# A PSUM buffer shared by feed-forward and spectral work: another engine frees it, and the spectral pieces stand at other places

## The chip, the cores and the metric

One core of one Trainium2 chip. The metric is the device time of the kernel in microseconds (us), median of several runs. PE is TensorE, PEld its weight loads, DVE VectorE, ACT ScalarE, POOL GpSimd, SP SyncE. Before and after are compared within the same rounds.

## The reference, cut to what matters

The reference returns an output and seven gradients of a gated mix of a spectral filter `a` and a GeGLU feed-forward block `b`:

```python
g = _sigmoid((x * gate_w).sum(-1, keepdims=True))
a = _A_ref(x, A_w_r, A_w_i)      # rfft2, times a complex weight, irfft2
b = _B_ref(x, B_w_gate, B_w_up, B_w_down)   # (gelu(x@w_gate) * (x@w_up)) @ w_down
return g * a + (1 - g) * b
# out: value, and by vjp the gradients of all inputs but B_x   (x: 2048 x 576, F = 4608)
```

The kernel has a first phase (18 groups of columns, 4 pairs of row blocks each: products z and x·w, the gate's elementwise work, weight gradients of an earlier group, and between them the spectral transforms as small "pieces") and a second phase of pure matrix products.

## The kernel before: the parts that matter

The PSUM tiles of the first phase make up eight banks, where a bank is 512 F32 per partition (a `[P, 2, 512]` tile is two). Four hold the x products (`ph`, two buffers of two banks), two hold weight gradients (`pw`), and the last two are one single buffer, `pz`. It serves z at the start of a pair and each spectral piece after the first group:

```python
pz = ps1.enter_context(tc.tile_pool(name="pz", bufs=1, space=PSUM))
...
def pftile():                       # PSUM of a spectral piece
    fctr[0] += 1
    if pw is None and fctr[0] % 2:  # first group only: a second buffer
        return pg.tile([P, 2, 512], F32, tag="pg", name="pf")
    return pz.tile([P, 2, 512], F32, tag="z", name="pf")
```

The last piece of the inverse transform (a product with the D table) read its two results from PSUM with ScalarE once and with VectorE twice:

```python
ev = unit([DF], F32, name="ev")                       # DF = 289
yo = unit([D], name="yo")
nc.scalar.activation(ev[:], yps[:, 0, :DF], ACT.Copy, scale=scale)
V.scalar_tensor_tensor(yo[:, 0:DF], yps[:, 1, :DF], scale, ev[:], op0=ALU.mult, op1=ALU.add)
V.scalar_tensor_tensor(yo[:, D - 1:DF - 1:-1], yps[:, 1, 1:DF - 1], -scale, ev[:, 1:DF - 1],
                       op0=ALU.mult, op1=ALU.add)
```

A pair of row blocks, from the second group on (`hs` are the halves of weight-gradient products, `fft_next()` emits one piece, `H_ew1`/`H_ew2` are the two parts of the gate's elementwise work):

```python
z, xy_full = H_mm(g, m)             # z into pz
xy = xy_full(0)                     # first x product
das = H_da(m, z)                    # four ScalarE reads free z
ta = H_ew1(xy)                      # ScalarE: q, xb, hu; VectorE: four instructions
for h in carry: h()
xy = xy_full(1)                     # second x product
fft_next()                          # first piece
tc_ = H_ew1(xy); H_ew2(g, 2 * m, ta, das[0])
hs[0]()
run_W(hs[1:], n - k, mid)           # other pieces by count, often the last one at the end
```

## Time and profile before

| | before |
|---|---|
| time, median (the runs that the prediction had) | 1579.02 us (1577.78 to 1581.86) |
| span of the profiled run | 1573.3 us |
| PE busy / idle | 1468.2 / 105.1 us |
| mean granted PE clock | 0.981 |

The lines of the page, of the stretches and of the waits are in the prediction below. They are read in this order: how busy PE is, in which stretch it is not, what it waits for there, and how one such wait comes about.

### The profile page before, as it was taken

How to read it: one execution, taken by the hardware profiler on the slowest of the kernel's cores; microseconds unless marked ns; L12 is line 12 of the kernel's file. 1: busy time of each engine (PE TensorE's matmuls, PEld its weight loads, DVE VectorE, ACT ScalarE, POOL GpSimd, SP SyncE). 2: the span in 40 equal slices, each digit the busy share in tenths (PEclk: the TensorE clock that was granted, in tenths of full speed). 3: DMA queues.
4: the chain of work that ended last, by engine and by line, in shares of the span. 5: the costliest groups of instructions: out<-in, count | busy, mean ns of one | idle time of the engine just before them, and what ended most of it. 6: DMA issues, size and time to landing. Idle time of an engine off the chain costs nothing.

```text
span 1573.3 us, 29838 instructions
## 1 busy us (share of the span) xinstructions
PE 1468.2 (93%) x11760; PEld 1074.2 (68%) x11760; DVE 844.5 (54%) x2243; ACT 685.5 (44%) x1355; POOL 22.3 (1%) x51
## 2 busy tenths in 40 slices
PE   7989999799999999989989888799998999999998
PEld 5657667567667666656656565576877777777776
DVE  6596676788767886655756556567113312121100
ACT  5576665566665766545655455466100000000000
POOL 1000000000000000000000000000000000000000
PEclk9999999899999999999999999999999999999999
DMA  5144434445444444432433334354999987778773
GB/s 181 50 120 114 119 106 124 122 120 157 125 131 124 122 118 119 121 111 77 122 103 111 107 91 114 100 144 122 257 203 217 203 167 163 161 168 159 157 152 70
DMA packets 503353, 210.47 MB, mean 134 GB/s; under 512 B 307595, under 2 KB 497068, under 8 KB 503212
## 3 DMA queue, kind: packets, MB, share of 16 engines
q1 hardware_dynamic: 499772, 202.83, 52.6%
q0 software_dynamic: 1632, 4.72, 1.0%
q8 instruction: 92, 1.51, 0.4%
q10 hardware_dynamic: 1808, 1.02, 0.2%
q14 instruction: 49, 0.40, 0.1%
HBM read 40.89 MB, written 93.82 MB: 86 GB/s over the span
## 4 chain that ended last, share of the span: by engine, by line
PE 56%; issue 23%; DVE 9%; ACT 5%; POOL 1%; DMA 1%; SPq 1%; POOLq 0%; DVEq 0%; ACTq 0%
PE xy L332 16%; PE wps L429 13%; PE z L320 9%; PE wps L412 5%; PE acc L909 3%; PE xy L327 2%; PE acc L951 2%; PE wps L442 2%; PE z L323 1%; PE pf L655 1%; PE pf L478 1%; ACT q L352 1%; DVE om L374 1%; DVE A L372 1%; ACT xb L353 1%
## 5 line engine op out<-in xcount | busy, mean ns | idle before, releaser
L332 PE MATMUL xy<-wgu,xT 128*128 128x512 bf16 x1152 | 264.8, 380 | 0.0
L951 PEld LDWEIGHTS <-pin 128*128 128x128 bf16 x2304 | 225.4, 98 | 56.8
L429 PEld LDWEIGHTS <-xn 128*128 128x128 bf16 x2304 | 225.8, 98 | 32.1 <-issue 0.2
L332 PEld LDWEIGHTS <-xT 128*128 128x128 bf16 x1152 | 106.9, 98 | 146.8 <-issue 32.1
L345 ACT ACTIVATE da<-z,omg 128x256 bf16<-128x256 f32 x288 | 113.3, 475 | 193.6 <-PE z L323 193.0
L320 PE MATMUL z<-wdT,dOT 128*128 128x256 bf16 x1152 | 150.3, 288 | 46.8 <-DVE yo L674 21.7
L355 DVE TENSOR_SCALAR s<-q 128x512 bf16<-128x512 bf16 x144 | 41.9, 291 | 237.3 <-ACT q L352 237.3
L320 PEld LDWEIGHTS <-dOT 128*128 128x128 bf16 x1152 | 116.7, 103 | 74.3 <-issue 31.5
L412 PE MATMUL wps<-dB,A 128*128 128x288 bf16 x1152 | 156.5, 286 | 0.0
L909 PE MATMUL acc<-wd_all,pin 128*128 128x288 bf16 x1152 | 143.7, 286 | 6.2 <-ACT f32t L914 4.5
L951 PE MATMUL acc<-wgT,pin 128*128 128x288 bf16 x1152 | 143.4, 286 | 0.0
L951 PE MATMUL acc<-wuT,pin 128*128 128x288 bf16 x1152 | 143.4, 286 | 0.0
L909 PEld LDWEIGHTS <-pin 128*128 128x128 bf16 x1152 | 112.6, 98 | 35.8 <-issue 5.7
L429 PE MATMUL wps<-dHg,xn 128*128 128x256 bf16 x1152 | 136.1, 274 | 0.0
L412 PEld LDWEIGHTS <-A 128*128 128x128 bf16 x1152 | 112.7, 98 | 29.8
L429 PE MATMUL wps<-dHu,xn 128*128 128x256 bf16 x1152 | 132.8, 273 | 0.0
L961 ACT COPY f32t<-acc 128x576 f32<-128x576 f32 x16 | 10.2, 639 | 249.1 <-PE acc L951 249.1
L352 ACT ACTIVATE q<-xy 128x512 bf16<-128x512 f32 x144 | 86.1, 598 | 65.5 <-PE xy L332 65.5
L963 DVE SCALAR_TENSOR_TENSOR f32t<-gwf,dlog,f32t 128x576 f32<-128x576 f32 x16 | 13.1, 818 | 186.6 <-ACT f32t L961 186.6
L364 ACT ACTIVATE om<-s 128x512 bf16<-128x512 bf16 x144 | 93.0, 646 | 3.3 <-DVE s L356 3.3
L365 ACT ACTIVATE s<-s 128x512 bf16<-128x512 bf16 x144 | 90.7, 630 | 4.6
L354 ACT CAST hu<-xy 128x512 bf16<-128x512 f32 x144 | 87.5, 608 | 0.0
(176 smaller groups left out, 1736.9 us busy)
## 6 DMA issues: line engine op xcount, KB each, us to landing
scr<-A SPq DMA_DIRECT2D x144, 128.0 KB, 1.8
scr<-dHg SPq DMA_DIRECT2D x144, 128.0 KB, 1.9
scr<-dHu SPq DMA_DIRECT2D x144, 128.0 KB, 1.9
out_dram<-dw SPq DMA_DIRECT2D x67, 128.0 KB, 2.1
wd_all<-in_B_w_down_dram SPq DMA_DIRECT2D x3, 1728.0 KB, 12.6
out_dram<-dwd SPq DMA_DIRECT2D x34, 144.0 KB, 1.9
scr_p<-Vt SPq DMA_DIRECT2D x32, 144.5 KB, 2.2
Vp<-scr_p SPq DMA_DIRECT2D x16, 289.0 KB, 3.1
```

Of the source, the lines that this page charges most:

```text
L320: nc.tensor.matmul(zo(t), lhsT=dOT[:, ci, t, :], rhs=wdT[:, ci, :], start=(t % 4 < 2 and ci == 0), stop=False)
L332: nc.tensor.matmul(xy[k][:, t % 2, :], lhsT=xT[:, ci, t, :], rhs=wgu[:, ci, :], start=False, stop=(ci == 3))
L345: nc.scalar.activation(da[:, tt, :], z[:, tt, k, :], ACT.Copy, scale=omg32[:, t:t + 1])
L352: nc.scalar.activation(q[:], hg, ACT.Square)
L354: nc.scalar.copy(hu[:], xy[:, :, FG:2 * FG])
L355: V.tensor_scalar(s[:], q[:], A_GELU, 1.0, op0=ALU.mult, op1=ALU.add)
L364: nc.scalar.activation(om[:], s[:], ACT.Sigmoid, scale=-2.0 * C_GELU)
L365: nc.scalar.activation(s[:], s[:], ACT.Sigmoid, scale=2.0 * C_GELU)
L412: nc.tensor.matmul(wps[:, :288], lhsT=tl(0, t)[:, fch * P:(fch + 1) * P], rhs=dB[:, t, h * 288:(h + 1) * 288], start=(t == 0), stop=(t == ...
L429: nc.tensor.matmul(wps[:, cc, :], lhsT=xn[:, t, (c0 + cc) * P:(c0 + cc + 1) * P], rhs=tl(k, t), start=(t == 0), stop=(t == T - 1))
L909: nc.tensor.matmul(bps[:, h, :288], lhsT=At[:, r, :], rhs=wd_all[:, fc, h * 288:(h + 1) * 288], start=(fc == 0), stop=(fc == NFC - 1))
L951: nc.tensor.matmul(xps[:, h, :288], lhsT=src[:, r, :], rhs=wT[:, h * 288:(h + 1) * 288], start=(k == 1 and f0 + r == 0), stop=(k == 2 and ...
```

## The change

The intent: z is freed by ScalarE alone and no longer by VectorE, whose queue is long (in the case at 681 us that the prediction shows, the gate's six instructions L371 to L376 ran ahead of VectorE's own two reads); and no piece stands right before the next z or right behind another piece. The core of the diff:

```diff
-                ev = unit([DF], F32, name="ev")
+                ev = unit([2, DF], F32, name="ev")
                 yo = unit([D], name="yo")
-                nc.scalar.activation(ev[:], yps[:, 0, :DF], ACT.Copy, scale=scale)
-                V.scalar_tensor_tensor(yo[:, 0:DF], yps[:, 1, :DF], scale, ev[:], ...)
-                V.scalar_tensor_tensor(yo[:, D - 1:DF - 1:-1], yps[:, 1, 1:DF - 1], -scale, ev[:, 1:DF - 1], ...)
+                nc.scalar.activation(ev[:], yps[:, :, :DF], ACT.Copy, scale=scale)
+                V.tensor_tensor(yo[:, 0:DF], ev[:, 0, :], ev[:, 1, :], op=ALU.add)
+                V.tensor_tensor(yo[:, D - 1:DF - 1:-1], ev[:, 0, 1:DF - 1], ev[:, 1, 1:DF - 1], op=ALU.subtract)
...
             das = H_da(m, z)
-            ta = H_ew1(xy)
+            q = H_q(xy)                       # only the first of the three ScalarE reads
+            if n:
+                fft_next()                    # first piece: between the two x products
+                n -= 1
+            ta = H_ew1(xy, q)
...
+                jobs = [(0, sig0)] * bool(carry) + carry + [(1.7, second)] + [(0, sig0)] * (not carry) + hs
+                us = sum(j[0] for j in jobs)
+                at, k, late = 0.0, 1, [sig1]
+                for w, f in jobs:             # w: 1.7 us for a w half or an x product, 1.0 for a d half
+                    if k <= n and at > 0 and at >= k * us / (n + 1) - 0.6:
+                        fft_next()
+                        k += 1
+                        if len(state) == 2 and late:
+                            late.pop()()      # second sigmoid block
+                    f()
+                    at += w
```

(Cut: `run_W` goes, every half carries its time, the first group keeps the order of its matmuls, where the first piece stood between the x products before too.)

More of the change, by code (lines that the diff above doesn't have):

```diff
@@ L347, in H_da, with H_q, H_ew1 @@
         return das
-    def H_ew1(xy):
-        xb, q, s, hu = (ewt(n) for n in ("xb", "q", "s", "hu"))
-        hg = xy[:, :, 0:FG]
-        nc.scalar.activation(q[:], hg, ACT.Square)
-        nc.scalar.copy(xb[:], hg)
+    def H_q(xy):
+        q = ewt("q")
+        nc.scalar.activation(q[:], xy[:, :, 0:FG], ACT.Square)
+        return q
+    def H_ew1(xy, q):
+        xb, s, hu = (ewt(n) for n in ("xb", "s", "hu"))
+        nc.scalar.copy(xb[:], xy[:, :, 0:FG])
         nc.scalar.copy(hu[:], xy[:, :, FG:2 * FG])
@@ L398, in W_units, with halves @@
         dwd_tiles, wp = {}, {}
-        def halves(f):
-            return [lambda: f(0), lambda: f(1)]
+        def halves(f, us):
+            return [(us, lambda: f(0)), (us, lambda: f(1))]
         def wtile(key):
@@ L422, in f @@
                     wst[0].dma_start(out_6[r0:r0 + P, :], dwd[:])
-            return halves(f)
+            return halves(f, 1.0)
         def u_dw(k, ov, c0):
@@ L435, in f @@
                 wst[0].dma_start(ov[:, c0:c0 + TPB, fsl], dw[:])
-            return halves(f)
+            return halves(f, 1.7)
         def tail(half):
@@ L449, in tail @@
             wst[0].dma_start(out_5[512:576, fsl], dw[HI, :])
+        tl_ = halves(tail, 1.0)
         w = [u_dw(k, ov, c0) for k, ov in ((1, o4v), (2, o5v)) for c0 in range(0, 4, TPB)]
@@ L452, in W_units @@
         if g == 0:
-            return [[w[0], halves(tail)], [w[1], d[0]], [d[1], d[2], d[3]], [w[2], w[3]], []]
-        return [[d[0]], [d[1], w[0]], [d[2], d[3], halves(tail)], [w[1], w[2]], w[3]]
+            return [[w[0], tl_], [w[1], d[0]], [d[1], d[2], d[3]], [w[2], w[3]], []]
+        return [[d[0]], [d[1], w[0]], [d[2], d[3], tl_], [w[1], w[2]], w[3]]
     side = []
@@ L669, in f @@
                                          start=(lc == 0), stop=(lc == 2))
-                ev = unit([DF], F32, name="ev")
+                ev = unit([2, DF], F32, name="ev")
                 yo = unit([D], name="yo")
-                nc.scalar.activation(ev[:], yps[:, 0, :DF], ACT.Copy, scale=scale)
-                V.scalar_tensor_tensor(yo[:, 0:DF], yps[:, 1, :DF], scale, ev[:], op0=ALU.mult, op1=ALU.add)
-                V.scalar_tensor_tensor(yo[:, D - 1:DF - 1:-1], yps[:, 1, 1:DF - 1], -scale, ev[:, 1:DF - 1],
-                                       op0=ALU.mult, op1=ALU.add)
+                nc.scalar.activation(ev[:], yps[:, :, :DF], ACT.Copy, scale=scale)
+                V.tensor_tensor(yo[:, 0:DF], ev[:, 0, :], ev[:, 1, :], op=ALU.add)
+                V.tensor_tensor(yo[:, D - 1:DF - 1:-1], ev[:, 0, 1:DF - 1], ev[:, 1, 1:DF - 1], op=ALU.subtract)
                 LD.dma_start(dv[:, i, :], yo[:])
@@ L752, in early_loads @@
         LD.dma_start(gwb[:], gate_w.partition_broadcast(P))
-    def run_W(hs, n, mid=None):
-        total = max(len(hs), 1)
-        k = 0
-        for j in range(total):
-            while k < n and k * total <= j * n:
-                fft_next()
-                k += 1
-            if mid and 2 * j >= total - 1:
-                mid()
-                mid = None
-            if j < len(hs):
-                hs[j]()
-        while k < n:
-            fft_next()
-            k += 1
     carry, pend = [], None
@@ L797, with sig0, second, sig1 @@
             das = H_da(m, z)
-            ta = H_ew1(xy)
+            q = H_q(xy)
[3 more added lines that the diff above has]
+            ta = H_ew1(xy, q)
+            state = []
+            def sig0():
+                H_ew2(g, 2 * m, ta, das[0])
+                side_work()
+                state.append(None)
+            def second():
+                xy = xy_full(1)
+                state.insert(0, H_ew1(xy, H_q(xy)))
+            def sig1():
+                H_ew2(g, 2 * m + 1, state[0], das[1])
+                side_work()
             if g == 0:
+                second()
                 fft_next()
-            for h in carry:
-                h()
-            carry = []
-            xy = xy_full(1)
-            k = 1 if n and hs else 0
-            if k or g == 0:
-                fft_next()
-            tc_ = H_ew1(xy)
-            H_ew2(g, 2 * m, ta, das[0])
-            def mid():
-                side_work()
-                H_ew2(g, 2 * m + 1, tc_, das[1])
-                side_work()
-            if hs:
-                hs[0]()
-            if g == 0:
-                fft_next()
-                mid()
-            else:
-                run_W(hs[1:], n - k, mid)
+                sig0()
+                fft_next()
+                sig1()
+            else:
+                jobs = [(0, sig0)] * bool(carry) + carry + [(1.7, second)] + [(0, sig0)] * (not carry) + hs
[3 more added lines that the diff above has]
+                    if k <= n and at > 0 and at >= k * us / (n + 1) - 0.6:
+                        fft_next()
+                        k += 1
[3 more added lines that the diff above has]
+                    at += w
+                while k <= n:
+                    fft_next()
+                    k += 1
+                if late:
+                    sig1()
+            carry = []
             if pr == 1:
@@ L866 @@
     wst[0] = nc.scalar
-    for h in carry + [h for us in pend[:4] for u in us for h in u] + pend[4]:
+    for _, h in carry + [h for us in pend[:4] for u in us for h in u] + pend[4]:
         h()
```

## The prediction

Also cut is the working by which the two VectorE sums would cost the same from SBUF as from PSUM, a change of nothing in part (1); the trace before did not show that. The 0.45 to 0.46 us under "What would show it" is what they took before (0.458 and 0.449).

> **What bounds the kernel now.** I read the page's busy shares first, then the busy time by stage, then what the TensorE waits for, then one stretch of the timeline.
>
> ```profile
> span 1573.3 us, 29838 instructions
> PE 1468.2 (93%) x11760; PEld 1074.2 (68%) x11760; DVE 844.5 (54%) x2243; ACT 685.5 (44%) x1355; POOL 22.3 (1%) x51
> ```
>
> TensorE (PE) is busy for 93% of the span, so the kernel can gain by matmul time or by the 105 us (1573.3 - 1468.2) in which PE stands still. The change removes no matmul. So the question is where those 105 us lie. The stretches below are the ones where the work changes: head and forward transform (to 225), the spectral middle (225 to 600), the inverse transform (600 to 1050), the pairs without spectral work, the second phase. Columns: stretch, its length, then busy time of PE, PEld, VectorE (DVE), ScalarE (ACT), GpSimd, then granted clock, DMA share, GB/s.
>
> ```profile
> 0.00:110.00 110.00, 91.51 (x810) 63.80 (x811) 77.16 (x202) 69.56 (x126) 4.39 (x18) 0.95 0.41 121
> 110.00:225.00 115.00, 112.98 (x901) 80.35 (x899) 79.40 (x225) 73.53 (x147) 0.00 (x0) 1.00 0.37 103
> 225.00:600.00 375.00, 353.56 (x2785) 247.56 (x2784) 290.28 (x774) 237.10 (x477) 0.00 (x0) 0.98 0.45 130
> 600.00:1050.00 450.00, 399.95 (x3084) 278.43 (x3083) 274.35 (x760) 247.13 (x501) 0.00 (x0) 0.96 0.38 107
> 1050.00:1110.00 60.00, 60.00 (x494) 44.31 (x492) 43.46 (x121) 34.99 (x71) 0.00 (x0) 1.00 0.52 133
> ```
>
> The inverse stretch loses 450 - 399.95 = 50.0 us and the middle 375 - 353.56 = 21.4 us. Where no spectral piece is interleaved (1050 to 1110) PE is never idle: the feed-forward part alone saturates it. So the spectral pieces bring the idle time. The waits of PE from 200 to 1100 us say how (total us, times, longest):
>
> ```profile
> PE z L320 <- DVE yo L674: 21.7, 12, 4.9
> PE pf L655 <- DVE yo L674: 17.7, 12, 4.1
> PE z L320 <- ACT Vt L618: 12.3, 4, 8.0
> PE pf L667 <- DVE yo L674: 4.4, 2, 4.0
> PE z L320 <- ACT ZT L658: 3.8, 4, 1.4
> ```
>
> All are waits for one buffer: z, two PSUM banks held once and no second pair, which the z product of each pair of row blocks and every spectral piece take in turn. 21.7 + 17.7 + 4.4 = 43.8 us are waits for the second VectorE instruction that reads an inverse D result; the other lines of that view add up to 27.7 us, nearly all for a ScalarE evacuation that had only just begun because the piece stood right before the next z. One case:
>
> ```profile
> 681.36 0.40 ACT L672 ACTIVATE ev<-pf 128x289 f32<-128x289 f32 x1
> 681.50 0.42 DVE L371 TENSOR_TENSOR xb<-xb,s 128x512 bf16<-128x512 bf16 x1
> ...
> 683.88 0.46 DVE L673 SCALAR_TENSOR_TENSOR yo<-pf,ev 128x289 bf16<-128x289 f32 x1
> ...
> 684.25 0.45 DVE L674 SCALAR_TENSOR_TENSOR yo<-pf,ev 128x287 bf16<-128x287 f32 x1
> ...
> 684.85 1.44 PE L655 MATMUL pf<-Btab,Vp 128*128 128x256 bf16 x6 [4.11 <-DVE yo L674]
> ...
> 687.17 3.57 PE L320 MATMUL z<-wdT,dOT 128*128 128x256 bf16 x16 [0.89 <-ACT ZT L658]
> ```
>
> ScalarE had its half at 681.76. VectorE still had to run the gate's L371 to L376, six elementwise instructions, ahead of its two, so the bank came free at 684.70, 2.9 us later. And then the 16 z matmuls took 3.57 us; undisturbed they take 1.9. The wait is followed by slow matmuls.
>
> [...] granted clock 0.50 from 685 to 690 us after the 4.11 us wait, likewise after the 8.0 us one. In windows of 5 us, busy time times (1 - clock) sums to 3.1 us in the middle and 11.8 us in the inverse stretch: a second cost of the same waits. [...] the trace has 406 (ev) and 639 (128x576 f32 to f32, line L961). [...] 759 ns for 576 elements in the trace (L965) [...].
>
> **The change, part by part.** (1) Evacuation. Thirty-two ACTIVATEs of 289 elements become 32 of 578: 32 x (0.64 - 0.41) = 7.4 us more ScalarE, spread over 450 us in which ScalarE is busy 247. Both VectorE sums now read SBUF[...]. The gain is that z comes free at the end of the ACTIVATE. In the case above that is 681.36 + 0.64 = 682.0 instead of 684.7, 2.7 of the 4.11 us; at 705.41 and 844.73 (waits 2.17 and 2.06, release 3.2 and 2.7 us earlier) the whole wait. I take 85% of 43.8, 37 us, for this part alone, and most of the slow matmuls with it.
> (2) Spacing. A pair of row blocks carries two or three pieces (157 slots over 61 pairs). Before, the last often came at the end of the pair, right before the z of the next one, or two stood about 1 us of matmul apart. Now one goes between the two x products and the others at even times. Worked through with durations of the trace for a pair with d, w pieces of the weight gradients, from the start of z: z matmuls to 2.1, tail rows to 2.6, first x product to 4.34; da (four ACTIVATEs) frees z at 3.9, so the first piece runs 4.34 to 5.08 without a wait; ScalarE does q to 5.15 and the piece 5.28 to 5.95. Second x product to 6.8, half a d to 7.8, second piece 7.8 to 8.45 (z free since 5.95); ScalarE still has q, xb, hu of the second half (to 8.6) and two sigmoids (to 9.85), so it evacuates at 9.85 to 10.65. Third piece at 11.2 to 11.9, evacuated by 13.0; the next z at 13.65. No wait of PE is left, the smallest margin is 0.5 us. For the first pair of a group, with the carried product ahead of the second x product, the last evacuation ends at about 13.6 and the next z is due at 13.7: no margin, so some waits of a few tenths there.
> (3) Order of the gate work. The second sigmoid block moves behind a piece; in the seven pairs after the last piece it moves to the end of the pair. ScalarE then has its two sigmoids 1.3 us before the next da is due, which is 2.3 us after the next z starts; it fits. In those seven pairs VectorE finishes about 1 us after the next da. No gain, little loss.
> Sum: idle 50.0 + 21.4 and slow clock 11.8 + 3.1 give 86.3 us at most (1579 - 86 = 1493). I leave 5 us in the inverse stretch. In the middle VectorE is busy 290 of 375 us and would be at 80% of a stretch of 360, and the 8.0 us wait went back to ScalarE waiting 6.5 us for VectorE products (buffers used in a ring), which spacing softens only; I leave 10 of 24.5 there. The forward part (6.3 us of z waits before 225 us) keeps its order in the first group: nothing. Gain 57 + 14 = 71, less 4 for small new waits: 67, so 1512 us.
>
> **Rivals.** (a) ScalarE takes the place of VectorE as the late releaser: its queue holds q, xb, hu and sigmoids ahead of a piece, up to 3 us. For it: in the case above the ACTIVATE itself came 1.6 us after the last matmul of its piece. Against: ScalarE is 55% busy in the inverse stretch, and the worked pair hides that delay. If the buffer came free 0.3 us late at each of the 128 middle and inverse pieces, that would leave some 38 us: 1545. (b) VectorE becomes the bound in the middle, since 12 product instructions per 8 pieces lie on top of the gate work. For it: 290 of 375 us; against: 375 - 21 = 354 still leaves 18% free. Then the middle gains nothing: 1526. (c) The waits hide something else, a transfer or the weight-gradient banks, and PE stays idle for that: DMA share is 0.38 to 0.45 there and PE waits for DMA only 1.1 us, for weight-gradient banks 0.4 us; I give it little, at most 20 us: 1532. (d) Everything goes: 1493.
>
> **Range and chances.** 1512 us, 1496 to 1540 for 8 in 10: the low end is nearly all of the 86 us, the high end is rival (a). Two per cent faster is 1547, a gain of 32 us; part (1) alone is worth 37 by the working above. Faster 0.89, same 0.10, slower 0.01.
>
> **What would show it.** In the changed kernel: PE busy at 440 or more of each 450 us in the inverse stretch, which shrinks to about 393; no wait of PE for yo; at most 20 us of waits for z in all, those left named ScalarE; clock 1.00 there; ScalarE's ev at 0.64 and the yo sums at 0.45 to 0.46; matmul counts equal and the second phase still 463 us. I would be wrong if waits of z for ev, ZT or Vt rise to 30 us or more (rival a), if VectorE is over 90% busy in the middle (b), or if PE is idle for other names (c).

## The result, and the profile after

| | before | after |
|---|---|---|
| time, median of 4 | 1580.44 us (1577.78 to 1582.66) | 1493.9 us (1492.21 to 1497.43) |
| span of the profiled run | 1573.3 us | 1490.4 us |
| PE busy / idle | 1468.2 / 105.1 us | 1450.0 / 40.4 us |
| mean granted PE clock | 0.981 | 0.993 |

The ratio is 0.9456, 95% interval 0.9432 to 0.948. (A ratio is the mean time of one kernel's runs over that of the other's of the same rounds, so not quite the ratio of the medians.) The gain of 86.5 us is larger than the 67 predicted, and the time lies below the stated range.

The head of the page after:

```profile
span 1490.4 us, 29909 instructions
PE 1450.0 (97%) x11760; PEld 1071.2 (72%) x11760; DVE 843.6 (57%) x2243; ACT 698.2 (47%) x1355; POOL 22.3 (1%) x51
```

The instruction counts are the same. PE idle fell by 64.7 us, and PE busy fell by 18.2 us although it does the same 11760 matmuls. Together that is the whole 82.9 us between the two spans.

Where: the same stretches of work in both kernels, cut at the first piece of the middle, the first of the inverse, the last of the inverse and the last z. First the kernel before (columns as in the prediction):

```profile
232.50:618.00 385.50, 364.85 (x2887) 257.81 (x2888) 293.19 (x782) 239.81 (x482) 0.00 (x0) 0.98 0.45 129
618.00:1015.50 397.50, 349.92 (x2699) 243.65 (x2697) 242.67 (x672) 219.08 (x443) 0.00 (x0) 0.97 0.37 104
1015.50:1093.00 77.50, 75.03 (x592) 52.26 (x592) 54.67 (x153) 45.33 (x94) 0.00 (x0) 0.96 0.55 138
```

Then the kernel after:

```profile
230.00:597.00 367.00, 360.01 (x2869) 255.43 (x2867) 293.15 (x781) 241.70 (x482) 0.00 (x0) 0.99 0.46 132
597.00:932.00 335.00, 335.00 (x2700) 241.27 (x2698) 238.07 (x663) 226.44 (x438) 0.00 (x0) 1.00 0.44 123
932.00:1010.00 78.00, 78.00 (x626) 54.03 (x624) 59.11 (x164) 50.27 (x104) 0.00 (x0) 1.00 0.60 149
```

Some 2700 matmuls of the inverse stretch took 397 us and now take 335, with PE busy throughout. By the times of the boundary instructions themselves (232.5, 618.1, 1014.8 and 1093.0 us before; 230.0, 596.7, 931.4 and 1006.6 after) the head gained 2.5 us, the middle 18.9, the inverse transform 62.0, the pairs behind it 3.0. The second phase (from 1131.7 of 1573.3, from 1045.3 of 1490.4) lost 3.5. The sum is 82.9. Between these boundaries the middle has 2888 matmuls before and 2866 after: some 22 of them, an estimated 2.8 us at 0.12 to 0.13 us each, moved into the head and the pairs behind, so that the middle itself gained nearer 16. In the inverse stretch the counts agree (2697 and 2698).

What PE still waits for (total us, times, longest; the first five lines):

```profile
PE tp L285 <- DMA xn<-in_A_x_dram: 5.0, 1, 5.0
PE acc L914 <- DMA pin<-scr: 4.2, 2, 2.1
PE z L320 <- ACT Vt L622: 4.1, 1, 4.1
PE acc L914 <- ACT f32t L919: 3.8, 5, 0.8
PE pf L496 <- DVE Vt L502: 3.7, 3, 1.2
```

The waits for yo are gone. One long wait for z is left, in the middle. The wait for xn stands at the start of the kernel and was there before (4.8 us). A piece with D results in the inverse stretch, to be set beside the case at 681 us that the prediction shows (timeline: start, length, engine, line, what):

```profile
679.81 0.29 PE L671 MATMUL pf<-At,ZT 128*128 128x289 bf16 x1
...
680.37 0.66 ACT L676 ACTIVATE ev<-pf 128x578 f32<-128x578 f32 x1
...
682.61 0.45 DVE L677 TENSOR_TENSOR yo<-ev 128x289 bf16<-128x289 f32 x1
...
682.98 0.45 DVE L678 TENSOR_TENSOR yo<-ev 128x287 bf16<-128x287 f32 x1
...
683.86 1.92 PE L320 MATMUL z<-wdT,dOT 128*128 128x256 bf16 x16
```

VectorE is as late as before: its sums end at 683.43, 2.4 us after ev. But z was free at 681.03, and the next z starts at 683.86 with no wait in brackets and takes 1.92 us (granted clock 1.00 from 683 to 688 us), against 3.57 in the case before. In this stretch the length of VectorE's queue no longer matters to PE. In the head some waits for VectorE remain (Vt L502, 3.7 us).

### The profile page after: what moved, and what is told of

Its sections match the earlier page's. It is cut to its first block, busy times and chain, and to the rows that moved or that the text cites. A ratio compares the mean times of both kernels' runs of the same rounds, so it can differ in the third digit from the quotient of the medians.

```text
span 1490.4 us, 29909 instructions
## 1 busy us (share of the span) xinstructions
PE 1450.0 (97%) x11760; PEld 1071.2 (72%) x11760; DVE 843.6 (57%) x2243; ACT 698.2 (47%) x1355; POOL 22.3 (1%) x51
## 4 chain that ended last, share of the span: by engine, by line
PE 66%; issue 23%; DVE 2%; SPq 1%; ACT 1%; DMA 1%; POOL 1%; POOLq 0%; ACTq 0%; DVEq 0%
PE wps L432 16%; PE xy L332 16%; PE wps L415 9%; PE z L320 8%; PE acc L914 3%; PE wps L445 2%; PE xy L327 2%; PE acc L956 2%; PE pf L671 2%; PE z L323 1%; PE pf L659 1%; PE pf L482 1%; POOL out_dram L971 1%; POOL out_dram L924 0%; DMA scr_p<-Vt 0%
## 5 line engine op out<-in xcount | busy, mean ns | idle before, releaser
L332 PE MATMUL xy<-wgu,xT 128*128 128x512 bf16 x1152 | 271.5, 380 | 0.0
L320 PE MATMUL z<-wdT,dOT 128*128 128x256 bf16 x1152 | 140.2, 276 | 5.9 <-ACT Vt L622 4.1
L320 PEld LDWEIGHTS <-dOT 128*128 128x128 bf16 x1152 | 112.6, 99 | 24.2 <-issue 9.6
L966 ACT COPY f32t<-acc 128x576 f32<-128x576 f32 x16 | 10.2, 639 | 249.1 <-PE acc L956 249.1
L919 ACT COPY f32t<-acc 128x576 f32<-128x576 f32 x16 | 10.2, 640 | 172.0 <-PE acc L914 172.0
```

The source lines that it names most:

```text
L320: nc.tensor.matmul(zo(t), lhsT=dOT[:, ci, t, :], rhs=wdT[:, ci, :], start=(t % 4 < 2 and ci == 0), stop=False)
L332: nc.tensor.matmul(xy[k][:, t % 2, :], lhsT=xT[:, ci, t, :], rhs=wgu[:, ci, :], start=False, stop=(ci == 3))
```

## The experiments

Two explanations compete for the gain: the earlier release (A in the texts below counts each part at its own worth) and the places of the pieces. The first two runs do one part alone. The differences in us that follow are between medians of runs; the ratios to the kernel before, each from its own rounds, say the same. The four runs of the changed kernel spread over 5 us (1492.21 to 1497.43), and runs 3 to 8 come from other rounds than it, so a difference of 5 us or less to it (runs 3, 6 and 7) is not clear of noise.

**1. The evacuation alone**, on the order of before.

```diff
 # kernel before, with only this
-                nc.scalar.activation(ev[:], yps[:, 0, :DF], ACT.Copy, scale=scale)
+                nc.scalar.activation(ev[:], yps[:, :, :DF], ACT.Copy, scale=scale)
 # and the two tensor_tensor sums on ev in place of the two scalar_tensor_tensor
```

> Only the evacuation of the inverse D results, on the old order of pieces. Theory A (the waits for yo are worth what the prediction's part (1) says, 37 us, plus about 9 us of slow clock behind them): 0.970 to 0.975 of the kernel before, about 1535 us; no wait of TensorE for yo left, the 27 us of waits for ScalarE evacuations still there. Rival B (the spacing is what counts and covers the late VectorE too): 0.99 or more.

Measured 1532.81 us, ratio 0.9698 (0.9672 to 0.9723): 48 us gained, as theory A has it. The inverse stretch went from 396.7 to 350.4 us (first and last inverse piece at 620.5 and 970.9), the middle did not gain (385.6 to 387.1). What PE waits for in this kernel:

```profile
PE z L320 <- ACT Vt L618: 12.3, 4, 8.0
PE z L320 <- ACT Y L484: 6.3, 5, 1.7
PE z L320 <- ACT ZT L658: 5.5, 4, 1.5
...
PE z L320 <- ACT ev L672: 3.6, 3, 1.3
```

No yo any more. The waits for ScalarE evacuations of the kernel before stand unchanged (Vt 12.3, Y 6.3), and ev joins them where a D piece is the last of its pair.

**2. The places without the evacuation**: the changed kernel with the old evacuation. The new order of the gate work, part (3) of the prediction, is in it too.

```diff
 # changed kernel, with only this taken back
-                nc.scalar.activation(ev[:], yps[:, :, :DF], ACT.Copy, scale=scale)
+                nc.scalar.activation(ev[:], yps[:, 0, :DF], ACT.Copy, scale=scale)
 # and the two scalar_tensor_tensor that read PSUM in place of the two tensor_tensor
```

> Only the new places of the pieces and the new order of the gate work; VectorE still reads the D results from PSUM. Theory A: the waits for ScalarE (27 us) go, but VectorE still frees z about 3 us after ev, which the worked pair with its 0.5 to 0.7 us of margin can't hide: 20 to 30 us of waits for yo remain, 0.965 to 0.975, about 1532 us. Rival B: 0.95 to 0.955, at most 10 us of waits for yo. If A's two halves (46 and 48 us) add up to more than the 86 us measured, they overlap.

Measured 1523.92 us, ratio 0.9632 (0.9602 to 0.9661): 57 us gained, a little more than theory A, far from B. The waits of PE in its inverse stretch:

```profile
PE pf L659 <- DVE yo L678: 10.1, 5, 2.5
PE z L320 <- DVE yo L678: 8.8, 6, 2.4
```

So 18.9 us of the 43.8 us of waits for yo remain, just under the 20 to 30 expected. The middle takes 367.3 us, as in the changed kernel (366.7): its gain is from the places and the order, not from the evacuation. The inverse takes 364.8. There the evacuation alone removes 46.3 us, the places without it 31.9 and both 62.0, so 16 us could be had by either. In the whole kernel 48 + 57 = 105 for 86.5.

**3 and 4. Taking the release back by a known amount.** ScalarE does each evacuation twice, which frees z later and loads ScalarE more.

```diff
 # 3: D results only; 4: all four kinds of evacuation of the middle and inverse
-                nc.scalar.activation(ev[:], yps[:, :, :DF], ACT.Copy, scale=scale)
+                for _ in range(2):
+                    nc.scalar.activation(ev[:], yps[:, :, :DF], ACT.Copy, scale=scale)
```

> The changed kernel with each of the 32 evacuations of D results on ScalarE done twice: z comes free about 0.56 to 0.65 us later at 32 pieces and ScalarE has 20 us more work. Theory A (the new order leaves slack of half a microsecond or more at nearly every piece, so the 0.3 us per piece of the prediction's rival (a) is hidden): within 4 us of the changed kernel, 1494 to 1498. Rival C (no slack, ScalarE's queue is on the path): 18 us or more, 1512.

> The changed kernel with all four kinds of spectral evacuation on ScalarE of the middle and inverse stretch done twice (128 instructions, about 80 us more ScalarE work, z free 0.6 to 0.75 us later at every piece). Theory A: up to 20 us, 1494 to 1514, because some third pieces have only 0.5 us of margin and ScalarE reaches some 80% busy. Rival C: 70 us or more, 1565.

Measured 1496.84 us (ratio 0.9472) and 1518.58 us (0.9605). Run 3 is 2.9 us slower than the changed kernel for 32 evacuations of 0.65 us, 0.09 us each and within the spread of the runs: the release had 0.65 us to spare nearly everywhere. The waits of its inverse stretch, 1.6 us in all, show it more safely than the time does:

```profile
PE pf L659 <- ACT ev L677: 0.8, 2, 0.4
PE pf L671 <- ACT ZT L662: 0.4, 1, 0.4
PE z L320 <- ACT ev L677: 0.4, 2, 0.2
```

Run 4 is 24.7 us slower for 128 evacuations, 0.19 us each (ACT busy 781.5 us), somewhat more than the 20 at most that A allowed, a third of what C asked. So there was slack for most of a doubling, and the changed kernel, which asks for none of it, has no ScalarE wait left in the inverse stretch.

**5. The first piece back behind the second x product**, all else as changed.

```diff
-            if n:
-                fft_next()
-                n -= 1
             ta = H_ew1(xy, q)
...
                 xy = xy_full(1)
+                if first[0]:
+                    fft_next()
                 state.insert(0, H_ew1(xy, H_q(xy)))
```

> The changed kernel with the first piece of a pair back behind the second x product, everything else as changed. Theory A (each place between pieces matters little as long as one evacuation fits, but in the first pair of a group two pieces now stand back to back): 5 to 20 us slower than the changed kernel, 1499 to 1514. Rival D (the place between the x products is the main part of the spacing): 30 us or more slower, 1524.

Measured 1509.28 us, ratio 0.9545: 15 us slower, within A. By stretches the head lost 6.4 us, the middle 3.6, the inverse 4.9. The 6.4 us of the head are no part of the gain: in the first group the first piece stood between the x products in the kernel before as well, and this run takes it away there too, so that it and the next one stand back to back. What the new place is worth is the 8.5 us of the middle and the inverse: part of the gain, not the main part.

**6. The first piece's evacuation behind q, xb and hu** on ScalarE, instead of behind q only.

```diff
             q = H_q(xy)
+            ta = H_ew1(xy, q)
             if n:
                 fft_next()
                 n -= 1
-            ta = H_ew1(xy, q)
```

> The changed kernel with the first piece's evacuation behind q, xb and hu on ScalarE, so that z comes free 1.2 us later at each first piece (61 of them). Theory A (slack of about 1.2 us before the second piece): 0 to 10 us slower, 1494 to 1504. Rival C (ScalarE's queue is on the path): 1.2 us at most first pieces, 40 us or more.

Measured 1497.08 us, ratio 0.9471: 3 us slower, within the spread of the runs. By stretches the head and the middle lost 1.6 us each and the inverse nothing (334.7 us again). The split of `H_q` from `H_ew1` is worth no more than that; in the inverse stretch the 1.2 us fit before the second piece, as A expected.

**7. Spaced by count.**

```diff
+                jobs = [(1.2 * (w > 0), f) for w, f in jobs]
                 us = sum(j[0] for j in jobs)
```

> The changed kernel with the pieces spaced by the number of jobs instead of their time (each job counted as 1.2). Theory A (any place with about 1.7 us of matmuls on each side does): within 6 us of the changed kernel. Rival E (the time weights are what makes the difference): 10 us or more slower.

Measured 1498.53 us, ratio 0.9484: 4.6 us slower, within A's 6 and hardly clear of noise. The exact times of the jobs matter little.

**8. The last piece at the end of the pair.**

```diff
-                    if k <= n and at > 0 and at >= k * us / (n + 1) - 0.6:
+                    if k < n and at > 0 and at >= k * us / (n + 1) - 0.6:
```

> The changed kernel with the last piece of each pair at the end of the pair again, right before the next z; the evacuation stays on ScalarE. Theory A (an end-of-pair piece costs its drain, evacuation and ScalarE's queue, 0.9 to 1.5 us, at some 50 of 61 pairs that end with a piece with matmuls): 45 to 75 us slower, 1540 to 1570, with as many us of waits of z for ScalarE. Rival F (the ScalarE evacuation alone makes the place unimportant): under 15 us.

Measured 1546.45 us, ratio 0.9784: 52.6 us slower than the changed kernel, within A's 45 to 75. (In pairs that have only this one piece left after the first, the second sigmoid block goes to the end as well, behind the piece's evacuation.) Its waits from the middle on:

```profile
PE z L320 <- ACT Vt L622: 12.5, 11, 5.2
PE z L320 <- ACT ZT L662: 10.6, 12, 0.9
PE z L320 <- ACT ev L676: 9.6, 13, 0.7
PE z L320 <- ACT Xx L558: 5.8, 8, 0.7
PE z L320 <- ACT Xg L560: 4.4, 6, 0.7
```

These are 50 waits and 42.9 us. This one place decides more than all other details of spacing. And it shows a cost that idle time does not: PE busy is 1459.0 us here, 9.0 us more than in the changed kernel, with the granted clock as high (0.994 against 0.993). Of these, 1.5 us lie in the second phase, which has no z. The rest, over 55 more waits for z in the whole run (57 against 2), is 0.14 us each. In the D piece at 702 us of this run a matmul is recorded for 0.29 us while the next one starts 0.12 us after it; in front of a wait the other 0.17 us would stand alone, and the profile would call them busy. That reading is an estimate from these two numbers; no run takes these ends away by themselves. (The "drain" of the expectation was the author's estimate too. What the trace shows of this piece: its last matmul is recorded to 702.88 us and z starts at 703.62, after a wait of 0.74 for ev; in the changed kernel an ev takes 0.65.)

**9 to 12. What is left.** The wait of 4.1 us in the middle of the changed kernel, and what stands before it in the timeline:

```profile
291.58 0.53 SPq L224 DMA_DIRECT2D wdT<-wdT  x1
...
292.20 0.53 SPq L623 DMA_DIRECT2D scr_p<-Vt  x1
...
294.57 0.64 ACT L622 CAST Vt<-pf 128x578 bf16<-128x578 f32 x1 [4.40 <-DMA scr_p<-Vt]
...
295.27 3.57 PE L320 MATMUL z<-wdT,dOT 128*128 128x256 bf16 x16 [4.12 <-ACT Vt L622]
```

ScalarE could not evacuate for 4.40 us because its output buffer, one of a ring, still waited for an earlier Vt to be written to DRAM, and that write (issued at 292.20) stood in SyncE's queue behind the weight loads of the next group (the last at 291.58). Run 10 issues these 32 writes from GpSimd. Run 11 takes up the other new wait, for `pin` in the second phase, and spreads six loads of transposed weights over more jobs. Run 12 does both, and run 9 is the changed kernel in the same rounds.

```diff
 # 10
-                LD.dma_start(dst[i], Vt[:])      # SyncE
+                ST.dma_start(dst[i], Vt[:])      # GpSimd
 # 11
-            if i > 1 and wT_loads:
+            if i > 1 and wT_loads and i not in (3, 6, 9):
```

> The changed kernel itself, in the same rounds as the next three, so that differences under 1% can be read: 0.945 of the kernel before, about 1494 us.

> The changed kernel with the 32 writes of the first inverse step to DRAM issued from GpSimd's queue instead of SyncE's, where they stood behind the weight loads of the next group. Theory A (the one 4.1 us wait of z that is left, with its slow matmuls, is a ScalarE evacuation held up by such a write through the ring of buffers): that wait goes, 4 to 9 us faster than the changed kernel, 1486 to 1490. Rival G (another buffer or a slower issue from GpSimd takes its place): within 2 us, or slower.

> The changed kernel with the six loads of transposed w_up in the second phase spread over jobs 2 to 10 instead of 2 to 7. Theory A (the two 2 us waits for pin in the second phase come from these loads): 3 to 6 us faster, 1488 to 1491, no wait for pin over 1 us. Rival H (the loads of w_down or the phase's own pins are the cause): no change.

> Both of the last two edits: 7 to 15 us faster than the changed kernel if they add, 1479 to 1487.

Measured: run 9 1494.27 us (0.9456), run 10 1490.62 (0.9431), run 11 1489.77 (0.9422), run 12 1483.09 (0.9382, 0.937 to 0.9395). Run 10 gained 3.7 us, just short of the 4 expected. All that PE waits for in its middle and inverse stretch is this line:

```profile
PE pf L550 <- DMA Vp<-scr_x: 1.3, 1, 1.3
```

Its waits for pin in the second phase came to 8.3 us in the profiled run, against 4.0 in run 9, which took back part of the gain in that run: against run 9 its middle took 358.2 us in place of 367.9, its second phase 450.7 in place of 444.9. In run 11 one wait for pin is left, 1.5 us long (none over 1 us was expected), and 4.5 us were gained. In run 12 none is left. It is 11.2 us faster than run 9, more than the 3.7 and 4.5 of the two edits alone: the middle took 357.8 us and the second phase 443.4, so that what run 10 lost there did not appear. These stretches are from one profiled run each. Run 12 is the fastest, correct like all others.

## Why the prediction was wrong, point by point

- **The bound** (PE idle for one buffer): right. With the waits gone the inverse stretch is 335.00 us busy of 335.00. One reading of the waits was too simple: the 27.7 us of the other lines (27.8 by the lines as printed) are not "nearly all" evacuations that had only just begun, since 8.0 of them are one wait in which ScalarE waited for VectorE's products, as the prediction says itself in its sum.
- **Part (1), 37 us and most of the slow matmuls:** right. Run 1 gained 48, of which 46.3 in the inverse stretch; the working had 37, and run 1's expectation 46 with the slow clock.
- **Costs of the instructions:** right. ev took 0.653 us (0.64 expected), the sums 0.456 and 0.452 (0.45 to 0.46 expected).
- **Part (2), the worked pair:** right, and more trustworthy than I took it for. It said that no wait is left. Then the sum said "I leave 5 us in the inverse stretch"; measured there is no idle time.
- **Part (3), the order of the gate work:** no loss appeared in the pairs without pieces; that stretch gained 3.0 us, its z waits and slow matmuls being gone. What the order alone is worth was not tried.
- **The step that failed is the sum.** The prediction had 57 us for the inverse and the pairs behind it; measured 62.0 + 3.0. It had 14 for the middle ("I leave 10 of 24.5 there"); measured 18.9. For the forward part it had "nothing", since that "keeps its order in the first group"; measured 2.5. The matmuls keep it, but ScalarE's order changed, and the waits for z and the pieces in the first group fell from 7.5 to 5.4 us (Y and Vt). Against this stood 4 us of new waits; measured 3.5, in the second phase and for pin. 8.0 + 4.9 + 2.5 + 0.5 make the 15.9 us by which the spans gained more than 67. The other 3.6 of the 19.5 lie between spans and medians: the profiled run before was a quick one.
- **Two errors are in that sum.** The first is the remainder of 5 us in the inverse stretch, put in without a wait that it would have been: nothing was left there. Runs 3 and 4 show what it overlooked, that a release 0.65 us later costs 0.09 us when it is one kind of piece and 0.19 when it is all. (The 10 for the middle were about right: 7.0 us idle and 2.7 us of slow clock remained there. More was gained all the same, in part because of the 22 matmuls that moved.) The second is the "at most". For the inverse stretch and the pairs behind it that was 50.0 + 11.8 = 61.8 us, and 65.0 were gained. It counted idle time and slow clock, and PE busy fell by more than the slow clock: in the inverse stretch by 14.8 us (349.5 to 334.7), where the slow clock, summed in windows of 5 us as the prediction did, was 10.0 us before and 0 after. The other 4.8 us are 0.15 at each of the 33 waits of that stretch, about the exposed end of a matmul in run 8. In the whole kernel the slow clock fell from 19.2 (18.8 to 19.8, by where the windows are cut) to 6.3 us, which is 12.9 of the 18.2. This division is an estimate from the traces.
- **Rival (d), everything goes, 1493 us:** the time came out there, in part by luck, since not everything went: what was left in the middle is made up for by gains that the sum did not count. The range ended 3 us above it. A range whose low end lies short of the worked schedule is not a range around it.
- **Rival (a)** was sized at 0.3 us for each of 128 pieces. It does not occur in the changed kernel, and run 4 had to double all evacuations to see 0.19. **Rival (b)** did not occur: VectorE is busy 293.15 of 367.00 us in the middle, as predicted (80%), and PE does not wait for it there. **Rival (c)** has a grain of truth: 4.1 us of z waits went back to a DMA in a queue, behind ScalarE's name.

## What to carry to other kernels

A buffer that is passed between engines can wait for the last of its readers: here z came free at 684.70 us, 2.9 us after ScalarE's read had ended, because six other instructions ran on VectorE ahead of its two reads. Let the reader be the engine with the shortest queue, and have the busier one work from a copy (48 us of 1581 by itself, run 1). A piece right before the next user of its buffer cost about 1 us at each of 50 places (run 8: 42.9 us of waits, 52.6 us in time), while the exact spacing elsewhere was worth little once one evacuation fitted (3 us in run 6, 4.6 us in run 7). And when a schedule worked through with measured durations leaves no wait, put the remainder that you add for safety into the range, not into the middle of it.
